# Transposing q and k by 64x64 products in four quarters of the array, and writing the tail of an expert's result row by one-column operations

## The chip, the cores and the metric

One core of one Trainium2 chip runs the kernel. The metric is the time on the device in microseconds (us) for one execution of the whole program: chunked attention, a layer of eight experts of which each token takes one, and a two-layer perceptron.

## The reference, cut to what matters

```python
# q, k, v: (8, 8, 576, 64) f32, standard normal * 0.1; chunks of 64 positions
scores = 64**-0.5 * (q_chunk @ k_chunk.T)          # 64x64 for each batch, head and chunk
attn = exp(scores - rowmax) / (rowsum + 1e-9)
x = (attn @ v_chunk) -> (4608 tokens, 512)         # heads side by side

expert = argmax(norm(x) @ norm(emb).T / tau)       # 8 experts
g = softmax(...)[expert]
x = g * (relu(x @ w1[expert]) @ w2[expert])        # 512 -> 1024 -> 512

h = x @ w_in                                       # 512 -> 2048
out = (h * sigmoid(1.702 * h)) @ w_out             # 2048 -> 512
```

## The kernel before, in words

The program runs through three stages on one core, which overlap a little at their borders.

**Attention (from the start to about 200 us).** The 4608 tokens are 36 tiles of 128; two tiles make a unit of 256 tokens. q and k arrive by unit (`load_qk`), with two neighbouring tokens on one partition, so a partition of a unit's tile holds, for each of 8 heads, 2 tokens of 64 numbers. `emit_T` turns a unit of k (on even steps) or of q (on odd steps) round: 8 f32 transposes of 128x128 on TensorE (L344) fill two PSUM tiles `tp` of tag A, which has two buffers, and four ScalarE copies (L349) of 64 partitions by 512 bring them to `kuT` or `quT`, two copies for each PSUM tile. A loop over steps n then issues, in an order written out by hand, work on several tiles at once. On TensorE a step holds the transposes of the next unit, the gate's products of an earlier tile (L491), the transposes of the attention result (L468), the scores (L371, 16 f32 products of 64x64, in four quarters of the array), the transposes of the probabilities (L394), and the product with v (L416). On ScalarE: the first two copies of L349, a square with row sum (L436), the other two copies, on every second step a copy of 128x1024 (L474), the copy of the transposed probabilities (L401), the exponential (L388). On VectorE: row maximum, subtraction, the division by the row sum (L424 to L428), the scale of the row and its f16 part (L442, L447, L452), the 128x1024 copy on the other steps (L476), and, dripped in between, the gate's small operations. GpSimd forms the rest of the f16 pair (L454, L455). SyncE's queue takes, in order, the loads of q and k, seven steps ahead, those of v, three batches ahead, and the store of the f16 pair (L461, from one of three buffers `xr`).

After the last tiles of a batch group the gate sorts tokens by expert. `find_scales` (L541 to L550) builds for the sorted rows an index `id_i` and a scale `sc_i`, once for the first 3 row tiles (128x3) and once for all (128x40).

**Experts (to about 672 us).** 39 row tiles of 128 sorted tokens are gathered and multiplied with the expert's two matrices, held as f16 pairs. `mm2_evac` (L1069) takes the result `py` out of PSUM: ScalarE sums its squares, VectorE makes a power-of-two scale of the row (L1077 to L1086), ScalarE writes the scaled f16 part (L1089), VectorE the rest (L1090), and beside the row goes a tail of four int32 numbers, which hold the token's index twice (L1078) and the row's scale as an f32 twice (L1093). The tail is written by two operations over 128x2 with a stride of two. The row of 2064 bytes goes to the array `ys` in memory.

**Perceptron (to the end).** The rows of `ys` are multiplied with `w_in` and `w_out` by a scheme of seven block products in place of eight; TensorE runs nearly without a pause.

Of the kernel before, what the change touches and what calls it, by code (L numbers as in the profile page):

```python
# [9 lines left out]
F32 = mybir.dt.float32  # L10
F16 = mybir.dt.float16
BF16 = mybir.dt.bfloat16
I32 = mybir.dt.int32
U32 = mybir.dt.uint32
AF = mybir.ActivationFunctionType
ALU = mybir.AluOpType
# [8 lines left out]
BIAS = 127  # L25
# [3 lines left out]
EXP_BITS = 0x7F800000  # L29
MAN_BITS = 0x007FFFFF  # L30
# [4 lines left out]
def kernel(  # L35
# [13 lines left out]
    nc = tc.nc  # L49
    B, H, S, D = q.shape  # L50
    NT, DM = out.shape
# [4 lines left out]
    HP = H // 2  # L56
# [5 lines left out]
    MAXT = NTILE + NE - 1  # L62
# [7 lines left out]
    const = ctx.enter_context(tc.tile_pool(name="const", bufs=1))  # L70
# [14 lines left out]
    YP = 2 * DM + 8  # L85
# [15 lines left out]
    QR = QU // 128  # L101
# [105 lines left out]
    )  # L207
    id_i = const.tile([128, MAXT], I32, name="id_i")
    sc_i = const.tile([128, MAXT], I32, name="sc_i")

    tau_sb = const.tile([128, 1], F32, name="tau_sb")
    nc.scalar.dma_start(out=tau_sb, in_=tau.partition_broadcast(128))
# [121 lines left out]
    qkT = {}  # L334

    def emit_T(u, nm):

        src = raw.pop((u, nm))
        qkT[u, nm] = att.tile([128, HP, QU], F32, tag=nm + "T", name=nm + "T", bufs=2)
        evacs = []  # L340
        for h2 in range(2):
            p = ps.tile([128, HP, 128], F32, tag="A", name="tp", bufs=2)
            for hp in range(HP):
                nc.tensor.transpose(  # L344
                    p[:, hp, :], src[:, 2 * hp + h2].rearrange("p r d -> p (r d)"), identF
                )
            dst = qkT[u, nm][h2 * 64:(h2 + 1) * 64].rearrange("p hp (c r) -> p hp r c", r=QR)
            evacs.append([
                lambda r=r, p=p, dst=dst: nc.scalar.activation(  # L349
                    out=dst[:, :, r], in_=p[r * 64:(r + 1) * 64], func=AF.Copy  # L350
                )
                for r in range(2)
            ])
        return evacs

# [189 lines left out]
    def scale_of(cols, got, parts_i):  # L545
        nc.vector.tensor_copy(parts_i[:, 0], got[:, 0])
        nc.vector.scalar_tensor_tensor(
            out=parts_i[:, 1], in0=got[:, 1], scalar=1024.0, in1=got[:, 2], op0=ALU.mult, op1=ALU.add
        )
        nc.vector.scalar_tensor_tensor(  # L550
            out=sc_i[:, cols], in0=parts_i[:, 0], scalar=21, in1=parts_i[:, 1],
            op0=ALU.logical_shift_left, op1=ALU.bitwise_or
        )

    def gate(bi):
# [510 lines left out]
    def mm2_evac(i):  # L1066
# [3 lines left out]
        ysq = mo.tile([128, DM], F16, tag="ysq", name="ysq", bufs=1)  # L1070
        s = mo.tile([128, 4], F32, tag="ys", name="ysc", bufs=2)
        si = s.bitcast(I32)
        c_i = sc_i[:, i:i + 1]
        tail = y[:, 2 * DM:YP].bitcast(I32).rearrange("p (a two) -> p a two", two=2)
        n = (YP - 2 * DM) // 4
        nc.scalar.activation(out=ysq, in_=p, func=AF.Square, scale=2.0 ** -20, accum_out=s[:, 0:1])
        nc.vector.tensor_scalar(si[:, 3:4], c_i, EXP_BITS, None, op0=ALU.bitwise_and)  # L1077
        nc.vector.tensor_copy(tail[:, :, 0], id_i[:, i:i + 1].to_broadcast([128, n]))  # L1078
        nc.vector.tensor_scalar(s[:, 0:1], s[:, 0:1], Y_MIN * 2.0 ** -40, None, op0=ALU.max)
        nc.vector.tensor_scalar(  # L1080
            si[:, 1:2], si[:, 0:1], 24, 23, op0=ALU.logical_shift_right, op1=ALU.logical_shift_left
# [1 line left out]
        nc.vector.tensor_scalar(  # L1083
            si[:, 1:2], si[:, 1:2], -1.0, float((BIAS + Y_TOP - 20) << 23), op0=ALU.mult, op1=ALU.add
        )
        nc.vector.scalar_tensor_tensor(  # L1086
            out=si[:, 2:3], in0=c_i, scalar=MAN_BITS, in1=si[:, 1:2], op0=ALU.bitwise_and, op1=ALU.bitwise_or
        )
        nc.scalar.activation(out=y[:, 0:DM], in_=p, func=AF.Copy, scale=s[:, 2:3])  # L1089
        nc.vector.scalar_tensor_tensor(  # L1090
            out=y[:, DM:2 * DM], in0=p, scalar=s[:, 2:3], in1=y[:, 0:DM], op0=ALU.mult, op1=ALU.subtract
        )
        nc.vector.scalar_tensor_tensor(  # L1093
            out=tail[:, :, 1], in0=si[:, 3:4].to_broadcast([128, n]), scalar=float(BIAS << 23),
            in1=si[:, 1:2].to_broadcast([128, n]), op0=ALU.add, op1=ALU.subtract,
        )
        if i < NSURE:
            nc.sync.dma_start(out=ys[i * 128:(i + 1) * 128, :], in_=y)
        elif i < SURE:
# [741 lines left out]
```

## Time and profile before

| | us |
|---|---|
| time, median of 3 runs | 1353.53 (1352.38 to 1356.58) |
| the profiled execution's own time | 1351.38 |
| its span, first to last instruction | 1349.4 |
| busy in the span: TensorE | 1246.7 (92%) |
| VectorE | 1048.0 (78%) |
| ScalarE | 732.8 (54%) |
| GpSimd | 718.4 (53%) |
| mean granted TensorE clock | 0.976 |

The shares are means over stages that differ much: ScalarE is busy for 54% of the whole span, but the slices of the first 150 us show it at eight or nine tenths, and TensorE, at nine tenths from 200 us on, is at seven there. So each part of the change is read in the stage in which its lines run. In the trace a product of two f32 operands stands as two rows on TensorE, a transpose of f32 as one.

### The profile page before, as it was taken

Reading aid. Unit: us, or ns where it says so; the run is one execution under the profiler, and the core shown is the slowest. Engines: PE = TensorE matmul, PEld = TensorE weight load, DVE = VectorE, ACT = ScalarE, POOL = GpSimd, SP = SyncE. Lnnn points to the kernel's source line nnn. Section 1 sums busy time; section 2 is a strip of 40 time slices with the busy share of each in tenths; the row PEclk is TensorE's granted clock in tenths of the full one; section 3 lists DMA queues with packets and bytes.
Section 4 is the critical chain, followed back from the end, with each engine's and each line's share of the span. In section 5 each row is a group of like instructions: output and inputs, shape, how many; then the busy total and the mean of one; then the engine's idle time right before and its main releaser. Section 6 shows DMA issues by size and latency. Waiting matters only on the chain. (4 is left out here: it accounts for less than half of the span.)

```text
span 1349.4 us, 35343 instructions
## 1 busy us (share of the span) xinstructions
PE 1246.7 (92%) x14192; PEld 1027.2 (76%) x14192; DVE 1048.0 (78%) x1872; ACT 732.8 (54%) x1301; POOL 718.4 (53%) x652
## 2 busy tenths in 40 slices
PE   6777767899999999999899999999999999999997
PEld 4666656677676666667588888888888888888886
DVE  4688888878988778886678696968687896968681
ACT  7899855235544545554463645545454645455452
POOL 1455543142444254543167575757667675757664
PEclk9999877999999999999999999999999999999999
DMA  9999635668665759885507162544526062534413
GB/s 197 233 242 230 160 129 131 181 181 229 191 182 174 212 161 274 266 253 133 151 15 212 58 183 99 129 154 94 188 39 226 19 205 77 157 125 125 157 42 116
DMA packets 218454, 213.62 MB, mean 158 GB/s; under 512 B 127320, under 2 KB 171352, under 8 KB 218272
## 3 DMA queue, kind: packets, MB, share of 16 engines
q1 hardware_dynamic: 204880, 184.17, 51.0%
q0 software_dynamic: 6000, 19.67, 4.3%
q10 hardware_dynamic: 7392, 7.36, 1.6%
q8 instruction: 114, 1.87, 0.6%
q14 instruction: 68, 0.56, 0.2%
HBM read 154.98 MB, written 36.52 MB: 142 GB/s over the span
## 5 line engine op out<-in xcount | busy, mean ns | idle before, releaser
L1536 PEld LDWEIGHTS <-wS 128*128 128x128 f16 x3024 | 296.2, 98 | 48.9 <-issue 9.7
L1029 PEld LDWEIGHTS <-w1HL 128*128 128x128 f16 x3744 | 216.9, 99 | 24.1 <-DVEq L962 6.7
L1029 PE MATMUL ph<-xTm,w1HL 128*128 128x128 f16 x3744 | 223.0, 222 | 12.2 <-DVEq L962 5.5
L1064 PE MATMUL py<-w2HL,hT 128*128 128x512 f16 x912 | 203.9, 379 | 6.0 <-DVEq L962 3.4
L1064 PEld LDWEIGHTS <-hT 128*128 128x128 f16 x936 | 89.9, 98 | 109.1 <-issue 8.0
L1089 ACT ACTIVATE y<-py,ysc 128x512 f16<-128x512 f32 x38 | 26.1, 687 | 142.8 <-DVE ysc L1086 142.8
L1004 POOL DMA_INDIRECT xg<-xs,id_i x39 | 44.3, 1135 | 107.6 <-DMA xTm<-xg 70.0
L1536 PEld LDWEIGHTS <-w2HL 128*128 128x128 f16 x864 | 84.6, 98 | 10.6
L1536 PEld LDWEIGHTS <-w1HL 128*128 128x128 f16 x864 | 84.5, 98 | 9.8
L454 POOL TENSOR_TENSOR x<-x,sx_all 128x512 f32<-128x512 f32 x33 | 34.3, 1039 | 107.3 <-DVE rd L424 41.9
L1256 POOL TENSOR_TENSOR wS<-d_f,wS 128x512 f16<-128x512 f32 x28 | 37.0, 1339 | 73.4 <-ACT wS L1255 44.5
L1562 ACT ACTIVATE zA<-zA 128x512 f32<-128x512 f32 x72 | 45.3, 628 | 53.2 <-DVE zA L1559 26.9
L1403 POOL TENSOR_TENSOR w1HL<-zA,w1HL 128x512 f16<-128x512 f32 x36 | 48.5, 1346 | 43.6 <-ACT w1HL L1399 39.7
L1396 DVE TENSOR_TENSOR zA<-zA 128x512 f32<-128x512 f32 x72 | 65.6, 910 | 1.2
L1037 DVE SCALAR_TENSOR_TENSOR hT<-ph,hT 128x512 f16<-128x512 f32 x78 | 51.4, 684 | 14.8 <-ACT hT L1036 14.7
L1036 ACT ACTIVATE hT<-ph 128x512 f16<-128x512 f32 x78 | 44.2, 594 | 30.0 <-PE ph L1029 30.0
L1536 PE MATMUL pd<-stg,wS 128*128 128x256 f16 x456 | 54.5, 272 | 2.2 <-ACT stgB L1399 2.2
L1697 POOL DMA_INDIRECT out_dram<-hT,idc x36 | 35.4, 983 | 35.7 <-ACT hT L1692 32.6
L1536 PE MATMUL pa<-stg,wS 128*128 128x256 f16 x432 | 51.7, 273 | 1.5 <-ACT stgB L1399 1.5
L1090 DVE SCALAR_TENSOR_TENSOR y<-py,ysc,y 128x512 f16<-128x512 f32 x38 | 28.5, 751 | 28.8 <-ACT y L1089 28.8
L1536 PE MATMUL pb<-stg,wS 128*128 128x256 f16 x408 | 48.9, 272 | 1.5 <-ACT stgB L1399 1.5
L349 ACT ACTIVATE kuT<-tp 64x512 f32<-64x512 f32 x72 | 45.2, 628 | 8.8 <-PE tp L344 7.9
(408 smaller groups left out, 3134.4 us busy)
## 6 DMA issues: line engine op xcount, KB each, us to landing
ring<-wod SPq DMA_DIRECT2D x63, 1024.0 KB, 5.1
stg<-in_moe_w_dram SPq DMA_DIRECT2D x14, 1024.0 KB, 6.9
stgB<-in_moe_w_dram SPq DMA_DIRECT2D x14, 1024.0 KB, 6.8
ys<-y SPq DMA_DIRECT2D x39, 258.0 KB, 3.2
vt<-in_v_dram SPq DMA_DIRECT2D x64, 144.0 KB, 5.7
xs<-xr SPq DMA_DIRECT2D x36, 256.0 KB, 5.6
raw_o<-in_moe_w_in_dram SPq DMA_DIRECT2D x16, 512.0 KB, 4.3
raw_o<-in_moe_w_out_dram SPq DMA_DIRECT2D x16, 512.0 KB, 3.8
```

Source lines behind the costliest of these rows:

```text
L349: lambda r=r, p=p, dst=dst: nc.scalar.activation(out=dst[:, :, r], in_=p[r * 64:(r + 1) * 64], func=AF.Copy)
L1004: nc.gpsimd.indirect_dma_start(out=xg[:, :], out_offset=None, in_=src, in_offset=bass.IndirectOffsetOnAxis(ap=id_i[:, i:i + 1], axis=0),)
L1029: nc.tensor.matmul(p[:, f % 4], wt[:, c, fs], xT[:, a, :], start=(c == 0 and a == 0 and wt is w1H), stop=(c == KD - 1 and wt is w1L),)
L1036: nc.scalar.activation(out=hi, in_=p, func=AF.Relu)
L1037: nc.vector.scalar_tensor_tensor(out=lo, in0=p, scalar=0.0, in1=hi, op0=ALU.max, op1=ALU.subtract)
L1064: nc.tensor.matmul(p, hT[:, a, :], wt[:, c, :], start=st, stop=sp)
L1256: nc.gpsimd.tensor_tensor(out=L_, in0=f, in1=H_, op=ALU.subtract)
L1396: nc.vector.tensor_tensor(out=o, in0=x, in1=p, op=op)
L1403: eng.tensor_tensor(out=lo, in0=x, in1=hi, op=ALU.subtract)
L1536: nc.tensor.matmul(dst, lhs(a, k, ab), rhs(b, k), start=first and ab == abs_[0] and k == 0 and m == 0, stop=(k == n - 1 and m == 2), skip_ ...
L1562: nc.scalar.activation(out=z, in_=z, func=AF.Sigmoid, scale=1.702 * 2.0 ** -G_EXP)
L1697: disjoint("out", nc.gpsimd.indirect_dma_start(out=out[:, :], out_offset=bass.IndirectOffsetOnAxis(ap=id_t[j][0][:, 2 * h + t, 0:1], axis= ...
```

## The change

`emit_T` no longer uses transposes. It issues 32 f32 products of 64x64 a unit, each with 64 rows of the source as the operand that is multiplied from the left, transposed, and a 64x64 block of the identity on the right. The source's row half `a` picks the upper or lower half of the array's rows and the PSUM tile; the head's parity `h2` picks the half of its columns and so the half of the PSUM partitions. Both PSUM tiles are requested at the start. Two ScalarE copies of 128 partitions (L356) take the place of the four of 64; they read PSUM with a stride in the innermost dimension and write contiguously, where the old ones read contiguously and wrote with a stride of two. `find_scales` gets three more VectorE operations, which split the scale `sc_i` once for all rows into mantissa (`sc_m`) and exponent (`sc_e`). In `mm2_evac` these columns serve as operands of one-column operations: L1077 goes, L1086 becomes a product by the column `sc_m`, and the tail's two strided operations of two columns become twice two of one column.

```diff
--- before.py
+++ after.py
@@ -207,6 +207,8 @@
     )
     id_i = const.tile([128, MAXT], I32, name="id_i")
     sc_i = const.tile([128, MAXT], I32, name="sc_i")
+    sc_m = const.tile([128, MAXT], I32, name="sc_m")
+    sc_e = const.tile([128, MAXT], F32, name="sc_e")
 
     tau_sb = const.tile([128, 1], F32, name="tau_sb")
     nc.scalar.dma_start(out=tau_sb, in_=tau.partition_broadcast(128))
@@ -338,18 +340,22 @@
         src = raw.pop((u, nm))
         qkT[u, nm] = att.tile([128, HP, QU], F32, tag=nm + "T", name=nm + "T", bufs=2)
         evacs = []
-        for h2 in range(2):
-            p = ps.tile([128, HP, 128], F32, tag="A", name="tp", bufs=2)
-            for hp in range(HP):
-                nc.tensor.transpose(
-                    p[:, hp, :], src[:, 2 * hp + h2].rearrange("p r d -> p (r d)"), identF
+        p = [ps.tile([128, QR, HP, 64], F32, tag="A", name="tp", bufs=2) for _ in range(2)]
+        for hp in range(HP):
+            for r in range(QR):
+                for a in range(2):
+                    rows = slice(a * 64, (a + 1) * 64)
+                    for h2 in range(2):
+                        nc.tensor.matmul(
+                            p[a][h2 * 64:(h2 + 1) * 64, r, hp, :], src[rows, 2 * hp + h2, r, :],
+                            identF[rows, rows], start=True, stop=True,
+                        )
+        for a in range(2):
+            dst = qkT[u, nm][:, :, a * 128:(a + 1) * 128].rearrange("p hp (i r) -> p hp i r", r=QR)
+            evacs.append([
+                lambda a=a, dst=dst: nc.scalar.activation(
+                    out=dst, in_=p[a].rearrange("p r hp i -> p hp i r"), func=AF.Copy
                 )
-            dst = qkT[u, nm][h2 * 64:(h2 + 1) * 64].rearrange("p hp (c r) -> p hp r c", r=QR)
-            evacs.append([
-                lambda r=r, p=p, dst=dst: nc.scalar.activation(
-                    out=dst[:, :, r], in_=p[r * 64:(r + 1) * 64], func=AF.Copy
-                )
-                for r in range(2)
             ])
         return evacs
 
@@ -550,6 +556,13 @@
         nc.vector.scalar_tensor_tensor(
             out=sc_i[:, cols], in0=parts_i[:, 0], scalar=21, in1=parts_i[:, 1],
             op0=ALU.logical_shift_left, op1=ALU.bitwise_or
+        )
+        nc.vector.tensor_scalar(
+            sc_m[:, cols], sc_i[:, cols], MAN_BITS, BIAS << 23, op0=ALU.bitwise_and, op1=ALU.bitwise_or
+        )
+        nc.vector.tensor_scalar(sc_e[:, cols].bitcast(I32), sc_i[:, cols], EXP_BITS, None, op0=ALU.bitwise_and)
+        nc.vector.tensor_scalar(
+            sc_e[:, cols], sc_e[:, cols].bitcast(I32), float(BIAS << 23), None, op0=ALU.add
         )
 
     def gate(bi):
@@ -1070,12 +1083,10 @@
         ysq = mo.tile([128, DM], F16, tag="ysq", name="ysq", bufs=1)
         s = mo.tile([128, 4], F32, tag="ys", name="ysc", bufs=2)
         si = s.bitcast(I32)
-        c_i = sc_i[:, i:i + 1]
-        tail = y[:, 2 * DM:YP].bitcast(I32).rearrange("p (a two) -> p a two", two=2)
-        n = (YP - 2 * DM) // 4
+        tail = y[:, 2 * DM:YP].bitcast(I32)
         nc.scalar.activation(out=ysq, in_=p, func=AF.Square, scale=2.0 ** -20, accum_out=s[:, 0:1])
-        nc.vector.tensor_scalar(si[:, 3:4], c_i, EXP_BITS, None, op0=ALU.bitwise_and)
-        nc.vector.tensor_copy(tail[:, :, 0], id_i[:, i:i + 1].to_broadcast([128, n]))
+        for a in range(0, tail.shape[1], 2):
+            nc.vector.tensor_scalar(tail[:, a:a + 1], id_i[:, i:i + 1], 0, None, op0=ALU.bitwise_or)
         nc.vector.tensor_scalar(s[:, 0:1], s[:, 0:1], Y_MIN * 2.0 ** -40, None, op0=ALU.max)
         nc.vector.tensor_scalar(
             si[:, 1:2], si[:, 0:1], 24, 23, op0=ALU.logical_shift_right, op1=ALU.logical_shift_left
@@ -1083,17 +1094,15 @@
         nc.vector.tensor_scalar(
             si[:, 1:2], si[:, 1:2], -1.0, float((BIAS + Y_TOP - 20) << 23), op0=ALU.mult, op1=ALU.add
         )
-        nc.vector.scalar_tensor_tensor(
-            out=si[:, 2:3], in0=c_i, scalar=MAN_BITS, in1=si[:, 1:2], op0=ALU.bitwise_and, op1=ALU.bitwise_or
-        )
+        nc.vector.tensor_scalar(s[:, 2:3], s[:, 1:2], sc_m[:, i:i + 1].bitcast(F32), None, op0=ALU.mult)
         nc.scalar.activation(out=y[:, 0:DM], in_=p, func=AF.Copy, scale=s[:, 2:3])
         nc.vector.scalar_tensor_tensor(
             out=y[:, DM:2 * DM], in0=p, scalar=s[:, 2:3], in1=y[:, 0:DM], op0=ALU.mult, op1=ALU.subtract
         )
-        nc.vector.scalar_tensor_tensor(
-            out=tail[:, :, 1], in0=si[:, 3:4].to_broadcast([128, n]), scalar=float(BIAS << 23),
-            in1=si[:, 1:2].to_broadcast([128, n]), op0=ALU.add, op1=ALU.subtract,
-        )
+        for a in range(1, tail.shape[1], 2):
+            nc.vector.tensor_scalar(
+                tail[:, a:a + 1], si[:, 1:2], -1.0, sc_e[:, i:i + 1], op0=ALU.mult, op1=ALU.add
+            )
         if i < NSURE:
             nc.sync.dma_start(out=ys[i * 128:(i + 1) * 128, :], in_=y)
         elif i < SURE:
```

On ScalarE's queue, in one step of the attention loop (a step for q, then one for k with its 128x1024 copy), before:

```order
L349 ACTIVATE quT<-tp 64x512 x2
L436 ACTIVATE sq,ss_all<-x 128x512
L349 ACTIVATE quT<-tp 64x512 x2
L401 ACTIVATE PT<-ptp 128x512
L388 ACTIVATE P<-P 128x512
L349 ACTIVATE kuT<-tp 64x512 x2
L436 ACTIVATE sq,ss_all<-x 128x512
L349 ACTIVATE kuT<-tp 64x512 x2
L474 ACTIVATE xTa<-sp_178 128x1024
```

and now:

```order
L356 ACTIVATE quT<-tp 128x4x128
L442 ACTIVATE sq,ss_all<-x 128x512
L356 ACTIVATE quT<-tp 128x4x128
L407 ACTIVATE PT<-ptp 128x512
L394 ACTIVATE P<-P 128x512
L356 ACTIVATE kuT<-tp 128x4x128
L442 ACTIVATE sq,ss_all<-x 128x512
L356 ACTIVATE kuT<-tp 128x4x128
L480 ACTIVATE xTa<-sp_180 128x1024
```

Every pair of copies has become one copy at the same place of the queue; nothing else has moved.

On TensorE's queue, around one unit's turning (the numbers tell apart the buffers), before:

```order
L371 MATMUL sp2_178<-kuT_500,quT_577 64x64 x16
L394 MATMUL ptp_829<-identF_85,P_722 128x128 x4
L416 MATMUL db_179<-vt1_92,PT_738 64x65 x16
L344 MATMUL tp_862<-identF_85,ku_511 128x128 x4
L344 MATMUL tp_867<-identF_85,ku_511 128x128 x4
```

and now:

```order
L377 MATMUL sp2_180<-kuT_430,quT_528 64x64 x16
L400 MATMUL ptp_702<-identF_85,P_593 128x128 x4
L422 MATMUL db_181<-vt0_91,PT_608 64x65 x16
L349 MATMUL tp_734<-identF_85,qu_390 64x64 x2
L349 MATMUL tp_735<-identF_85,qu_390 64x64 x2
L349 MATMUL tp_734<-identF_85,qu_390 64x64 x2
L349 MATMUL tp_735<-identF_85,qu_390 64x64 x2
```

(the last pair of rows stands eight times for a unit). Where one PSUM tile was filled and then the other, the two are now filled in turn, two products at a time, so the first products need both tiles free.

On VectorE's queue, one expert row tile's way out of PSUM, before:

```order
L1077 TENSOR_SCALAR ysc<-sc_i 128x1
L1078 COPY y<-id_i 128x2
L1079 TENSOR_SCALAR ysc<-ysc 128x1
L1080 TENSOR_SCALAR ysc<-ysc 128x1
L1083 TENSOR_SCALAR ysc<-ysc 128x1
L1086 SCALAR_TENSOR_TENSOR ysc<-sc_i,ysc 128x1
L1090 SCALAR_TENSOR_TENSOR y<-py_8698,ysc,y 128x512
L1093 SCALAR_TENSOR_TENSOR y<-ysc 128x2
```

and now:

```order
L1089 TENSOR_SCALAR y<-id_i 128x1 x2
L1090 TENSOR_SCALAR ysc<-ysc 128x1
L1091 TENSOR_SCALAR ysc<-ysc 128x1
L1094 TENSOR_SCALAR ysc<-ysc 128x1
L1097 TENSOR_SCALAR ysc<-ysc,sc_m 128x1
L1099 SCALAR_TENSOR_TENSOR y<-py_8622,ysc,y 128x512
L1103 TENSOR_SCALAR y<-ysc,sc_e 128x1 x2
```

One operation goes ahead of the scale, the two that wrote 128x2 are four of one column, and there are nine operations in place of eight. At the second `find_scales`, once in the program, three operations over 128x40 come in ahead of the evacuation of `hT`, now:

```order
L556 SCALAR_TENSOR_TENSOR sc_i<-got2i 128x40
L560 TENSOR_SCALAR sc_m<-sc_i 128x40
L563 TENSOR_SCALAR sc_e<-sc_i 128x40
L564 TENSOR_SCALAR sc_e<-sc_e 128x40
L1050 SCALAR_TENSOR_TENSOR hT<-ph,hT 128x512 x2
```

## Rows read from the trace of the kernel before

**Rows 1.** The span cut by stage: us, busy of each engine, clock, DMA share, GB/s

```profile
49.00:156.00 107.00, 84.67 (x2058) 67.75 (x2050) 92.08 (x285) 100.10 (x185) 57.59 (x60) 1.00 1.09 235
156.00:206.00 50.00, 31.05 (x643) 26.28 (x634) 41.08 (x131) 31.88 (x61) 23.85 (x25) 0.69 0.35 118
280.00:672.00 392.00, 376.76 (x4169) 272.59 (x4166) 320.79 (x548) 192.44 (x330) 160.72 (x134) 1.00 0.69 200
```

**Rows 2.** DMA of 49 to 156 us, then of 156 to 206: queue, and one issue's landing

```profile
DMA packets 54988, 25.12 MB, mean 235 GB/s; under 512 B 28522, under 2 KB 52120, under 8 KB 54966
...
xs<-xr SPq DMA_DIRECT2D x22, 256.0 KB, 6.4
...
xs<-xr SPq DMA_DIRECT2D x8, 256.0 KB, 2.0
```

**Rows 3.** Waits of 49 to 156 us: total us, times, longest

```profile
PE tp L344 <- ACT quT L349: 8.0, 10, 0.8
...
PE tp L344 <- ACT kuT L349: 6.2, 9, 0.8
DVE xr L452 <- DMA xs<-xr: 5.4, 4, 3.0
```

**Rows 4.** Groups by line, 49 to 156 us: busy us, mean ns | idle before, releaser

```profile
L349 ACT ACTIVATE kuT<-tp 64x512 f32<-64x512 f32 x44 | 27.7, 629 | 0.5
L349 ACT ACTIVATE quT<-tp 64x512 f32<-64x512 f32 x42 | 26.4, 628 | 0.5
...
L401 ACT ACTIVATE PT<-ptp 128x512 f32<-128x512 f32 x22 | 13.1, 595 | 0.6 <-PE ptp L394 0.4
```

**Rows 5.** Line L1261, a ScalarE reader with stride two: ns, minimum, median, maximum

```profile
L1261 ACT ACTIVATE d_t<-raw_o x32: 656/672/689, 265.4 to 599.7; 128x512 f32<-128x512 f32 x32
```

**Rows 6.** The span cut into 20 us (columns as in Rows 1)

```profile
80.00:100.00 20.00, 15.22 (x376) 12.17 (x374) 15.89 (x51) 17.87 (x35) 13.71 (x16) 1.00 1.12 245
100.00:120.00 20.00, 15.58 (x370) 12.45 (x371) 17.84 (x58) 19.31 (x36) 8.81 (x8) 1.00 1.15 252
```

**Rows 7.** Timeline, 155 to 192 us: start, us, instruction [idle before]

```profile
159.55 0.21 PE L596 MATMUL gb<-g_oh,tri 128*128 128x64 f16 x1 [3.37 <-DVE g_oh L586]
...
162.01 1.95 PE L344 MATMUL tp<-identF,ku 128*128 128x128 f32 x8
...
166.85 1.09 PE L344 MATMUL tp<-identF,qu 128*128 128x128 f32 x8
...
169.12 0.69 PE L371 MATMUL sp<-kuT,quT 64*64 64x64 f32 x32
```

**Rows 8.** Timeline, second scales: start, us, instruction [idle before]

```profile
265.08 0.26 DVE L550 SCALAR_TENSOR_TENSOR sc_i<-got2i 128x40 int32<-128x40 int32 x1
...
266.65 1.66 PE L1029 MATMUL ph<-xTm,w1HL 128*128 128x128 f16 x21 [1.65 <-DVEq L962]
```

**Rows 9.** Tile ysc, one-column operation: ns, minimum, median, maximum

```profile
L1079 DVE TENSOR_SCALAR ysc<-ysc x39: 139/146/155, 242.0 to 665.1; 128x1 f32<-128x1 f32 x39
```

**Rows 10.** Line L1078 (columns as in Rows 9)

```profile
L1078 DVE COPY y<-id_i x39: 153/159/4056, 242.0 to 661.6; 128x2 int32<-128x2 int32 x39
```

**Rows 11.** Groups by line, 280 to 672 us (columns as in Rows 4)

```profile
L1078 DVE COPY y<-id_i 128x2 int32<-128x2 int32 x35 | 24.0, 687 | 0.0
```

**Rows 12.** Timeline, evacuation after a change of weights: start, us, instruction [idle before]

```profile
552.03 0.62 DVE L1078 COPY y<-id_i 128x2 int32<-128x2 int32 x1
...
553.12 0.32 DVE L1086 SCALAR_TENSOR_TENSOR ysc<-sc_i,ysc 128x1 int32<-128x1 int32 x1
...
555.24 0.29 PE L1029 MATMUL ph<-xTm,w1HL 128*128 128x128 f16 x2 [1.91 <-ACTq L962]
```

**Rows 13.** Waits of 280 to 672 us: total us, times, longest

```profile
PE ph L1029 <- DVEq L962: 3.9, 6, 0.8
PE ph L1029 <- ACTq L962: 3.4, 3, 1.9
...
PE py L1064 <- DVEq L962: 3.4, 4, 1.1
```

## The prediction, made before the changed kernel ran

> **What bounds the kernel now.** I read the table of stages first, then for the stages touched the groups by line, the transfers and the waits. From 49 to 156 us ScalarE is busy for 100.10 of 107 us, VectorE for 92.08, TensorE for 84.67, at a granted clock of 1.00 [rows 1]: the reader is to see that ScalarE sets the pace there, and that two others stand close behind it. Behind these stands a third limit. In the same 107 us the queues move 25.12 MB at 235 GB/s, and a store of 256 KB lands after 6.4 us, where in the next stage it takes 2.0 [rows 2]: the transfers are queued up, and VectorE waits four times, once for 3.0 us, until an earlier store has freed the buffer that it writes [rows 3]. From 280 to 672 us TensorE is busy for 376.76 of 392 us [rows 1], and only what ends its waits is worth time. What moves less than 0.3%, some 4.06 us, can't be told from no change; so 1349.47 and 1357.59 are the borders of "same".
>
> **The copies.** Removed in 49 to 156 us: 44 and 42 copies at 629 and 628 ns, 54.1 us of ScalarE, or 1.257 us a pair [rows 4]. Added: 43 copies of 128 partitions over the same 512 columns. No row shows one with their stride. Below, a copy of PSUM of the same size without stride takes 595 ns [rows 4]; above, a ScalarE read with a stride of two takes 672 [rows 5]. That the old ones, with a strided write and half the partitions, took 629 tells that partitions are free and strides cheap. I take 610, nearest to the row that has the same source and size: 43 x 0.610 = 26.2 us, so ScalarE is relieved of 27.9 us (25.2 to 28.5). Its 100.10 falls to 72, and it is no longer the bound.
>
> What is late next decides the gain. VectorE keeps its 92.08 us, so not more than 14.9 us can go. The transfers keep their 25.12 MB: at the 245 GB/s of the 20 us from 80 to 100 us they take 102.5 us, at the 252 of the next 20, 99.7 [rows 6], against 107 now. Loads are issued seven steps ahead and stand behind stores and v in SyncE's queue, so a faster step asks earlier for the same bytes, and only the empty places between them can be filled. The stage's gain thus lies between 0 (235 GB/s is all that this mix of small pieces gives) and 7.3 us (252 throughout). I take 245, the stretch in which ScalarE was busy least, 17.87 of 20 us: 25.12 / 0.245 = 102.5, a gain of 4.4 us. The buffers of the stores let the computation end somewhat closer to the last load; I take 1.0 us, between 0 and the longest wait of 3.0.
>
> **The products on TensorE.** A unit's eight transposes took 1.09 us; 32 rows of 64x64 products, the same quarters in turn, took 0.69 [rows 7]. A product f32 is two rows, so the 32 new ones are 64 rows. Twice 0.69 is the upper bound, 1.38 us. The lower: one product alone lasts 0.21 [rows 7], the other 0.48 are eight groups of four rows at 0.06; 0.21 + 16 x 0.06 = 1.17. I take 1.17: 0.08 more a unit, with some 22 units 1.8 us (to 6.4) on an engine that idles for 22.3 of 107 us. Of that idle time 8.0 and 6.2 us ended with a copy of L349 [rows 3], which now ends earlier; the first products of a unit do need both PSUM tiles, but the second tile's copy is over 0.65 us sooner, more than the half turn of 0.55 that now starts behind it. Cost nothing while VectorE or the queue paces; 1.8 to 6.4 us if TensorE did.
>
> **156 to 206 us.** Here the clock is 0.69 and VectorE busy 41.08 of 50 us, ScalarE 31.88 [rows 1]: the copies are off the path. A unit's turn at the low clock takes 1.95 us [rows 7]; by 1.17/1.09 it grows by 0.14, twice: +0.3. The three scale operations over 128x3, 0.15 each, fall into VectorE's 8.9 idle us.
>
> **find_scales over 128x40.** Three operations beside L550's 0.26 us stand ahead of the L1037 for which TensorE then waits 1.65 us [rows 8]. A wait of that kind is lengthened by all of them: 3 x 0.18 = +0.5 us (0.45 to 0.8; 0 if another releases it).
>
> **The evacuation.** L1078 has a median of 159 ns and a maximum of 4056, in 280 to 672 us a mean of 687: 24.0 - 35 x 0.159 = 18.4 us of VectorE in stretched copies; the one-column L1079 never took over 155 in 39 [rows 9, 10, 11]. The new tail has the one-column form, so the stretches go and three small ones are added after the row. That is worth TensorE's time only where it waits for VectorE. After a change of weights it does: the copy took 0.62 and L1086 0.32 ahead of the scaled row, and the next product came 1.91 us late [rows 12]. There 0.46 + 0.16 us go; I count that place and one like it without L1086's part, 0.46: -1.1. Against it: ahead of the scale two operations stand where two stood, behind the row two for one, 0.15 us more; at seven changes of expert that is 1.0, of which I take half, since not each waits: +0.5. Net -0.6. The upper bound of a gain is all that TensorE waits there for these queues, 3.9 + 3.4 + 3.4 = 10.7 us [rows 13]; the bound of a loss 1.0.
>
> The Trainium skill, "SBUF — State Buffer", section Who interferes with whom, speaks against this part: it lists the tensor_scalar among the operations that can take the pair of ports shared with GpSimd and be blocked for a whole instruction. By that rule the new operations would be stretched like the copy and the -1.1 would be lost; the 39 rows of L1079 with a maximum of 155 ns do not bear it out for one column.
>
> **Sum.** -4.4 - 1.0 + 0.3 + 0.5 - 0.6 = -5.2 us, and nothing in the last stage, whose code is the same. The profiled execution of 1351.38 would become 1346.2; the median of the runs is 2.15 above the profiled time, so the forecast is 1348.3 us.
>
> **Rivals.**
> 1. *The queue takes it all.* 235 GB/s is what the queue gives with 28522 of 54988 packets under 512 bytes [rows 2]; ScalarE then simply waits for VectorE, and VectorE for the stores. For it: the landing of 6.4 us. Against: 245 and 252 in slices with the same work. Only +0.3 + 0.5 - 0.6 and up to 1 us are left: about 1352.7. Chance 0.25.
> 2. *VectorE sets the pace and the queue yields.* The step shortens until VectorE, 92.08 us, fills the stage but for some 5 us, as ScalarE now but for 6.9: 107 - 97 = 10 us, with the small terms 1343.5. For it: the queue may be full only because loads are asked for seven steps ahead. Against: the wait for stores. Chance 0.17.
> 3. *The clock of 156 to 206 us rises.* Its fall follows pauses of TensorE, as the 3.37 us at 159.55 [rows 7]. If products in the place of transposes kept it up, 0.62 of the stretch, the share that a mean of 0.69 between levels of 1 and 0.5 gives, would go at the upper level: 0.62 x 31.05 = 19.3 us busy become 10.8 by 1.95/1.09. Half of the 8.5 lies on the path: -4.2, so 1344.1. Against: the pauses that end with VectorE stay. Chance 0.05. The Trainium skill, "TensorE: Matmul & The Clock Gate", Part 4: PE-mode transpose, says that transposes do not count as busy for the clock, which would make this so; the trace's clock of 1.00 from 49 to 156 us, with eight transposes and more a step, lies against its strength.
> 4. *Slower: the clock of 49 to 156 us falls.* With ScalarE out of the way TensorE's short waits may run together into longer ones, for VectorE or a late load, as those before 159.55. At the low level its rows last 1.79 times as long (1.95 for 1.09). Its 22.3 idle us are used up once a third of the stage is at that level (84.67 x 0.79 x 0.33 = 22); from there each further tenth costs 6.7 us. At half the stage: 33.4 - 22.3 = +11, 1364. For it: the next stage does just this. Against: 1.00 now, and a shorter step gives denser work. Chance 0.08.
> 5. *The change does not do what it says.* If PSUM read with a stride in the innermost place made a copy cost 1.04 us or more, ScalarE would win under 10 us and the queue's gain shrink to about nothing: 1353. Against: 672 ns for the other stride. Chance 0.05.
>
> **How the numbers follow.** The forecast has 0.40, with a range of its own of 1345 to 1351.5 (the term of the queue between -7 and -1.5). Faster than 1349.47: 0.7 of its 0.40, rivals 2 and 3, 0.22, together 0.50. Same: 0.3 of 0.40, nearly all of rivals 1 and 5, 0.26: 0.38. Slower: rival 4 with tails of 1 and 5, 0.12. The range of 8 in 10: 1341.5 below, where half of rival 2 is left out, to 1355.5 above, where rival 4 and some of 1 are.
>
> **What would show it.** In the profile after: one copy a PSUM tile of 595 to 672 ns, 43 in the stage; ScalarE busy under 80 us in 49 to 156 and waiting for VectorE or TensorE; the end of the stage 4 to 6 us earlier with 240 to 250 GB/s; the turn of a unit at 1.17 to 1.38 us; more waits of VectorE for stores than 5.4 us; one-column tails that never exceed 160 ns; VectorE's busy time in the expert stage some 25 us lower with TensorE's waits nearly as before. The forecast is wrong if GB/s stay at 235 (rival 1), if the stage shortens by 8 us or more (rival 2), or if the clock of either stage differs by over 0.05 (rivals 3 and 4).

## The result, and the profile after

The changed kernel took 1365.67 us (median of four runs, 1360.17 to 1368.15) against 1355.05 before (1352.38 to 1357.32): a ratio of 1.0073 with a 95% interval of 1.0047 to 1.0099, so some 10 us slower. The forecast was 1348.3, between 1341.5 and 1355.5, faster at 0.50. It was wrong in sign. The profile shown below is of the fastest of the four runs (1360.17 us), 5.5 us under their median, so it shows rather less of the loss than a middle run would.

The table of stages of the changed kernel, whose columns are those of [rows 1], for the main part of the attention, for its end and for the expert stage:

```profile
49.00:156.00 107.00, 81.08 (x2832) 69.50 (x2831) 79.30 (x243) 64.14 (x129) 51.85 (x56) 0.90 0.92 212
156.00:206.00 50.00, 34.12 (x1165) 29.59 (x1165) 42.08 (x144) 25.89 (x52) 21.20 (x23) 0.86 0.31 91
...
280.00:672.00 392.00, 376.34 (x4220) 271.34 (x4221) 299.79 (x592) 192.04 (x327) 160.66 (x135) 1.00 0.73 209
```

ScalarE fell from 100.10 to 64.14 us of 107 [rows 1]. But VectorE fell too, from 92.08 to 79.30, the transfers from 235 to 212 GB/s: in the same 107 us the kernel did less of its work, and no engine is near its limit. 39 of the new copies stand in these 107 us where 43 pairs of the old ones stood; for the work of 43 ScalarE would take some 71 us, an estimate from these two numbers. The groups by line of this stage (busy us, mean ns | idle before, releaser) show the copies and what TensorE did:

```profile
L422 PE MATMUL db<-vt,PT 64*64 64x65 f32 x608 | 16.1, 245 | 5.4 <-issue 4.7 <-DVE x L434 0.7
L377 PE MATMUL sp<-kuT,quT 64*64 64x64 f32 x608 | 15.3, 238 | 6.4 <-issue 6.4
L349 PE MATMUL tp<-identF,ku 64*64 64x64 f32 x640 | 14.3, 239 | 2.2 <-issue 2.2
...
L349 PE MATMUL tp<-identF,qu 64*64 64x64 f32 x576 | 12.4, 230 | 3.9 <-issue 3.2 <-ACT kuT L356 0.7
...
L356 ACT ACTIVATE quT<-tp 128x512 f32<-128x512 f32 x20 | 11.9, 594 | 2.7 <-PE tp L349 2.6
L356 ACT ACTIVATE kuT<-tp 128x512 f32<-128x512 f32 x19 | 11.2, 587 | 5.8 <-PE tp L349 5.7
```

A copy of 128 partitions takes 587 and 594 ns, two of the old ones took 1257 [rows 4]. Where TensorE waited for these copies before, 8.0 and 6.2 us [rows 3], it now waits for "issue": for nothing that the profile shows. The waits of TensorE from 0 to 215 us (total us, times, longest):

```profile
PE tp L349 <- issue: 9.5, 9, 1.9
PE db L422 <- issue: 7.2, 6, 2.1
PE sp L377 <- issue: 6.4, 3, 2.6
PE ptp L400 <- issue: 3.1, 1, 3.1
PE gb L497 <- issue: 1.7, 1, 1.7
```

27.9 us in all. They fall on five different lines, the new products and old ones alike, and in the middle of a line's products. This is one of them in the timeline (start, us, instruction): a step's 32 score rows, which run for 0.69 us in one piece in [rows 7], stop after 19 of them for 2.61 us.

```profile
82.16 0.56 PE L377 MATMUL sp<-kuT,quT 64*64 64x64 f32 x19
85.32 0.45 PE L377 MATMUL sp<-kuT,quT 64*64 64x64 f32 x13 [2.61 <-issue]
85.33 0.31 PEld L377 LDWEIGHTS sp<-kuT,quT 64*64 64x64 f32 x12 [2.74 <-issue]
```

What ends them shows when all of TensorE's rows of the trace (products, weight loads and the rows of its sequencer) are counted from the start of the program. Each of the 15 pauses over 0.8 us in which it waited for issue comes at the same remainder of that count to 256, give or take one row. Nine of them:

```
goes on at us   pause us   rows since the last one listed
        36.6      1.9
        42.1      2.1        256
        52.6      2.4        512
        74.5      1.7       1280
        79.9      1.8        256
        85.3      2.6        256
        95.4      1.7        512
       114.7      3.1       1024
       124.8      1.7        512
```

From 30 to 215 us there are 21 pauses over 0.8 us in all, and these 15 stand at that remainder; before there are 22, and no remainder has more than two. The page of the profile lists a queue for instructions. Its row in the changed kernel (packets, MB, share):

```profile
q8 instruction: 129, 2.11, 0.7%
```

and in the kernel before:

```profile
q8 instruction: 114, 1.87, 0.6%
```

Each packet has 16384 bytes, 64 for each of 256 instructions. One of them starts at 82.5 us and lands at 83.7; TensorE goes on at 85.3. So it is in all 15 pauses: TensorE goes on 1.3 to 1.8 us after such a packet has landed. TensorE's program comes in pages of 256 instructions, it had used up one before the next was there, and waited. Between 30 and 150 us a page was fetched every 4.78 us in the mean (single ones 3.5 us apart), before every 6.89. In this stretch TensorE crosses into a new page 25 times, and each time exactly one page has been fetched since the crossing before: no more than one is held ahead. The trace also shows where the 4.78 us go. By the medians a fetch starts 2.0 us after a crossing, its packet takes 1.3 us, and a TensorE that stands waiting goes on 1.5 us after the landing. The Trainium skill, "Runtime: NRT & Kernel Launch", section Instruction fetch mechanics, gives the same page of 16 KiB or 256 instructions, and holds that fetching is mostly hidden; the first agrees with this trace, the second does not here.

Why more instructions: the whole page counts 16208 products of TensorE where 14192 were, 2016 more, each with its weight load: 4032 instructions over 36 units, 112 a unit. The last score product starts at 214.3 us (199.6 before), the first expert row is scaled 14.8 us later, the last expert row 10.6 later, the program ends 9.0 later in the profiled executions: 15 us lost in the attention, and in these two profiles some 4 won back in the experts.

In the expert rows the new operations never meet a stretch (tile ysc, then L1089: ns, minimum, median, maximum):

```profile
L1103 DVE TENSOR_SCALAR y<-ysc,sc_e x78: 202/205/207, 258.9 to 677.9; 128x1 int32<-128x1 int32 x78
...
L1097 DVE TENSOR_SCALAR ysc<-ysc,sc_m x39: 213/214/215, 257.3 to 676.2; 128x1 f32<-128x1 f32 x39
```

```profile
L1089 DVE TENSOR_SCALAR y<-id_i x78: 136/146/157, 256.6 to 672.1; 128x1 int32<-128x1 int32 x78
```

VectorE has 21 us less to do from 280 to 672 us, 299.79 for 320.79 [rows 1]. Those that take a column as their second operand last 205 and 214 ns, not 150.

### The profile page after: what moved, and what is told of

The parts are those of the page before. It is cut to its first block, busy times and chain, and to the rows that moved or that the text cites. A ratio compares the mean times of both kernels' runs of the same rounds, so it can differ in the third digit from the quotient of the medians.

```text
span 1358.4 us, 39310 instructions
## 1 busy us (share of the span) xinstructions
PE 1250.9 (92%) x16208; PEld 1038.9 (76%) x16208; DVE 1025.6 (76%) x1917; ACT 685.6 (50%) x1229; POOL 718.1 (53%) x652
## 5 line engine op out<-in xcount | busy, mean ns | idle before, releaser
L1042 PEld LDWEIGHTS <-w1HL 128*128 128x128 f16 x3744 | 213.2, 98 | 22.7 <-DVEq L975 8.4
L1042 PE MATMUL ph<-xTm,w1HL 128*128 128x128 f16 x3744 | 218.9, 220 | 11.5 <-DVEq L975 7.4
L1077 PE MATMUL py<-w2HL,hT 128*128 128x512 f16 x912 | 204.3, 379 | 5.9 <-DVEq L975 2.3
L1077 PEld LDWEIGHTS <-hT 128*128 128x128 f16 x936 | 89.9, 98 | 109.2 <-issue 8.5
L1545 PEld LDWEIGHTS <-w1HL 128*128 128x128 f16 x864 | 84.6, 98 | 9.8
L1050 DVE SCALAR_TENSOR_TENSOR hT<-ph,hT 128x512 f16<-128x512 f32 x78 | 51.6, 686 | 26.7 <-ACT hT L1049 26.6
L1412 POOL TENSOR_TENSOR w1HL<-zA,w1HL 128x512 f16<-128x512 f32 x36 | 48.5, 1348 | 41.7 <-ACT w1HL L1408 41.7
L384 DVE TENSOR_REDUCE mx<-sp 128x8 f32<-128x512 f32 x36 | 24.8, 688 | 47.0 <-PE sp L377 47.0
```

Of the source, the lines that this page charges most:

```text
L1042: nc.tensor.matmul(p[:, f % 4], wt[:, c, fs], xT[:, a, :], start=(c == 0 and a == 0 and wt is w1H), stop=(c == KD - 1 and wt is w1L),)
L1050: nc.vector.scalar_tensor_tensor(out=lo, in0=p, scalar=0.0, in1=hi, op0=ALU.max, op1=ALU.subtract)
L1077: nc.tensor.matmul(p, hT[:, a, :], wt[:, c, :], start=st, stop=sp)
L1412: eng.tensor_tensor(out=lo, in0=x, in1=hi, op=ALU.subtract)
L1545: nc.tensor.matmul(dst, lhs(a, k, ab), rhs(b, k), start=first and ab == abs_[0] and k == 0 and m == 0, stop=(k == n - 1 and m == 2), skip_ ...
```

## The experiments

Theory I: instruction pages; the new turn has too many instructions for their supply. Theory P: the products themselves, by their quarters, by the two PSUM tiles that they hold at once, or by the clock. Theory E: the new expert rows are at fault. Theory Q is the forecast's own third limit, the data queue. Experiments that were timed together share the runs of the kernel before; a gain or loss in us is the ratio's distance from one, times their median. "Last scores" is the start of the last score product in the profiled execution (199.6 us before).

**1. The attention's part alone.** Against the changed kernel:

```diff
-    sc_m, sc_e and their three operations in find_scales; one-column tail in mm2_evac
+    find_scales and mm2_evac as before
```

> The products and the 128-partition copies alone, the expert rows as before. Theory I (instruction pages): TensorE now gets 128 instructions a unit for the turn where it got 16, and its stream comes in pages of 256 instructions that arrive more slowly than it uses them; its pauses put down to 'issue' stand at whole multiples of 256 instructions after one another. The last scores end about 15 us later than before (199.9), the whole time is 13 to 16 us over before. Theory E (expert rows): if the new tail and scales were at fault, this kernel would be 4 to 8 us faster than before, as forecast.

1371.62 us, ratio 1.0141 (1.0117 to 1.0164): 19 us slower, last scores at 218.9. TensorE's waits from 0 to 215 us:

```profile
PE tp L347 <- issue: 13.9, 12, 2.5
PE sp L375 <- issue: 9.8, 4, 4.5
PE db L420 <- issue: 7.5, 7, 1.8
```

15 of its 20 pauses over 0.8 us stand at one remainder to 256, the same as in the changed kernel. The loss lies here. It is larger than theory I had said, and in the profile 4 us more than the changed kernel's, whose attention has the same code; one pause of 4.5 us is the plainest difference. Which run was profiled explains much of these 4 us (this one lies 1.7 us under its median, the changed kernel's 5.5), but not why the medians differ; that was not found.

**2. The rows' part alone.** Against the changed kernel:

```diff
-    emit_T: 32 products of 64x64, two copies of 128 partitions
+    emit_T: 8 transposes of 128x128, four copies of 64 partitions
```

> The expert rows and scale columns alone, the turn by transposes as before. Theory I: nothing of the loss is here; the stretched copies go, 4 to 5 us are gained between the first and the last row tile, 1349 to 1351. Theory E: 8 to 12 us slower than before. The forecast's own term: 0.1 us faster.

1350.92 us, ratio 0.9984 (0.9972 to 0.9996): 2.2 us faster, by the interval 0.5 to 3.8. From the scaling of the first expert row to that of the last it took 420.6 us, before 423.0: a gain in the place where theory I had it, but half of the 4 to 5 us expected. Theory E falls.

**3 and 4. The products for k alone, for q alone.**

```diff
-        (the products)
+        if nm == "ku":          # experiment 4: "qu"
+            (the products, two copies)
+        else:
+            (the transposes, four copies)
```

> The changed kernel, with the products for k alone; q by transposes and four copies as before. A pair of steps has then 144 instructions for turning in place of 32 (before) or 256 (changed). Theory I: about 240 instructions a step against 300, at some 50 a us 4.8 us a step: the pages keep up, ScalarE is relieved by half, and attention ends at or ahead of before: last scores at 195 to 201 us, time 1341 to 1350. Theory P (the products themselves cost the time, by the quarters, the two tiles held at once or the clock): half of the loss stays, last scores at about 207 us, time about 1357.

> The same with the products for q alone, k by transposes. Steps that turn k carry the 128x1024 copy on ScalarE, steps that turn q do not, so the relief falls on the lighter step. Theory I: pages keep up as in the half for k, but the gain is smaller, last scores at 197 to 202 us, time 1344 to 1351. Theory P: last scores at about 207 us, time about 1357.

For k: 1353.09 us, ratio 0.9999 (0.9980 to 1.0018), last scores at 201.9. For q: 1357.08, ratio 1.0026 (1.0014 to 1.0037), last scores at 210.3. Both missed: theory I had both gain, theory P had both at about 207. The waits of the kernel with q alone:

```profile
PE db L437 <- issue: 7.4, 5, 2.5
PE sp L392 <- issue: 5.7, 3, 2.4
PE tp L350 <- issue: 1.9, 3, 1.1
```

With one smaller wait that is 15.6 us; with k alone it is 8.5. The mean over two steps, by which I had reckoned, is not what counts when no more than one page is held ahead: a step of some 300 instructions is held up, and one of 184 beside it can't lend it time. With k alone the heavy stream falls on the step that ScalarE's 128x1024 copy makes long anyway; with q alone it falls on the short one. That reading fits both and was not tested apart.

**5 and 6. The same TensorE time, many instructions or few.** Both are edits of the kernel before.

```diff
 # experiment 5, emit_S
-        for hp in range(HP):
+        for hp in [i for _ in range(3) for i in range(HP)]:
 # experiment 6, emit_T and emit_PT
-            for hp in range(HP):
+            for hp in [i for _ in range(2) for i in range(HP)]:
-        for hp in range(HP):
+        for hp in [0, 1, 0, 1, 2, 3]:
```

> The kernel before, with the 16 score products of each step issued three times over into the same place: 128 instructions more a step for TensorE and about 1.4 us (two times 0.69), nothing else. Theory I (instruction pages): over 300 instructions a step, at the changed kernel's 5.0 to 5.8 us for them; pauses put down to issue at multiples of 256; last scores at 214 to 230 us as in the changed kernel or later, time 1367 to 1385. A theory by TensorE's time alone: 5.2 us a step where 5.0 were, last scores at 203 to 210, time about 1360, and no pauses of issue.

> The kernel before, with ten more 128x128 transposes a step (each unit turned twice over, two of the four transposes of the probabilities repeated): the same 1.4 us of TensorE as the score products issued thrice, but 20 instructions where these are 128. Theory I: no pauses of issue, last scores at 203 to 212 us, at least 8 us ahead of the kernel with the scores issued thrice. TensorE's time alone: the same as that kernel within 3 us.

Experiment 5: 1385.81 us, ratio 1.0241 (1.0224 to 1.0258), 33 us slower, last scores at 234.8, just over the far end of what theory I had said. Its waits:

```profile
PE sp L371 <- issue: 12.3, 11, 2.5
PE db L416 <- issue: 8.2, 6, 2.3
```

11 of its 14 pauses over 0.8 us stand at one remainder to 256, give or take two rows. Its stage:

```profile
49.00:156.00 107.00, 86.53 (x2733) 74.49 (x2723) 72.58 (x218) 82.57 (x151) 45.00 (x46) 0.97 0.90 207
```

Experiment 6: 1352.83, ratio 0.9997 (0.9981 to 1.0014), last scores at 202.0, no wait for issue. Its stage:

```profile
49.00:156.00 107.00, 103.91 (x2238) 91.56 (x2229) 92.17 (x284) 100.49 (x185) 56.81 (x59) 1.00 1.10 236
```

TensorE is at 103.91 of 107 us, 19.2 more than before [rows 1], and nothing is lost; with the instructions it is 33 us. In these two kernels `emit_T`'s copies, the tiles and the ScalarE load are those of before. This decides for the number of instructions, and against TensorE's time. It doesn't clear the form of the product, since experiment 5 adds quartered ones. What clears it is the count: the pauses come at the same remainder to 256 whether the next row is a quartered product (L371, L416), a 128x128 transpose (one of L344 here, one of L400 in the changed kernel) or a product of the gate (L497 there).

**7. The turn kept, other instructions taken away.** An edit of the changed kernel.

```diff
 def emit_S(t):
     u, tt = divmod(t, QR)
+    if t >= 2:
+        return
```

> The changed kernel, with the scores computed for the first two tiles alone; later tiles use those, so the attention is left out in part, and tokens go to other experts: only the attention stage is compared, by the last product with v. TensorE gets 64 instructions and 0.69 us a step less; the turning products and their copies stay. Theory I: 235 instructions a step, 4.6 to 4.8 us, the pauses of issue fall from about 28 us to under 8, and the last product with v ends at 200 to 212 us (before 214, changed 228). Theory P (the turning products themselves): pauses stay, the last product with v ends after 222.

1353.09 us, a time that can't be compared, as tokens go to other experts. The last product with v starts at 210.7 us, where it was 214.0 before and 228.1 in the changed kernel:

```profile
L424 PE MATMUL db<-vt,PT x1152: 217/218/367, 25.0 to 210.7; 64*64 64x65 f32 x192
```

All the loss of the attention is gone with 64 instructions a step less, with all the quartered turning products and both tiles in place. The scores' time on TensorE and the waits for them went too; experiment 6 speaks against the first, the second was not tested apart. Of waits for issue 15.7 us are left, twice what I had said, 13.3 of them before turning products; the five over 0.8 us stand at the same remainder to 256.

**8. Less data beside the pages.** An edit of the changed kernel, in `issue_v`.

```diff
-            nc.sync.dma_start(out=dst, in_=src)
+            if v_n[0] < H * NV:
+                nc.sync.dma_start(out=dst, in_=src)
```

> The changed kernel, with v loaded for the first three of eight batches alone (the others use these): 40 loads of 144 KB of 256-byte pieces are left out, about a quarter of the bytes and half the packets of the attention stage. Theory I with pages that stand behind data: a page comes sooner, the stage from 49 us on loses 5 to 12 of its 15 us. Theory I with a fixed time for a page: last scores within 3 us of the changed kernel's 214.7. Theory Q (the data queue is the bound, in both kernels): the stage ends 15 us earlier or more, ahead of the kernel before.

1360.73 us, ratio 1.0051 (1.0034 to 1.0068), last scores at 215.3. The stage:

```profile
49.00:156.00 107.00, 83.62 (x2906) 71.92 (x2908) 78.18 (x239) 63.42 (x127) 51.02 (x54) 0.89 0.63 168
```

The share of the DMA engines fell from 0.92 to 0.63, and a page still came every 4.79 us (4.78). The pages are not slow because data stand in front of them, and the queue does not pace the changed kernel.

**9 and 10. Half the instructions, more TensorE time.** For k alone, or for k and q:

```diff
-  nc.tensor.matmul(p[a][h2 * 64:(h2 + 1) * 64, r, hp, :], src[rows, 2 * hp + h2, r, :], identF[rows, rows], ...)
+  nc.tensor.matmul(p[h2 * 64:(h2 + 1) * 64, hp, :], src[:, 2 * hp + h2, c, :], identF, ...)
```

> The changed kernel, with k turned by 16 products of all 128 rows, 64 columns wide, against the 128x128 identity: the same two copies of 128 partitions, but 64 instructions a unit in place of 128; q by transposes and four copies as before. TensorE works about 1.9 us on such a unit in place of 1.17. Theory I: a page of 256 instructions takes some 4.8 us whatever the data load, so a step of 235 instructions needs 4.4 to 4.6 us and is no longer held up: few pauses of issue (under 4 us), last scores at 193 to 198 us (before 199.9, rows alone 196.7), time 1344 to 1350. Theory P: as the half for k with 64x64 products, last scores 202 or later, time 1353 or more.

> The same for k and for q: every step has about 235 instructions for TensorE, against 300 in the changed kernel, and its ScalarE is relieved as fully as in the changed kernel. Theory I: 4.6 to 4.9 us a step, by the pages and by TensorE's own 4.7; pauses of issue under 10 us; last scores at 190 to 200 us, time 1340 to 1352. Theory P: the loss stays, last scores after 208.

Experiment 9: 1350.71 us, ratio 0.9973 (0.9961 to 0.9986), last scores at 201.0, waits for issue 1.0 us. Experiment 10: 1350.91, ratio 0.9973 (0.9962 to 0.9984), last scores at 202.8. The stage of experiment 10:

```profile
49.00:156.00 107.00, 102.30 (x2578) 88.21 (x2576) 91.10 (x281) 72.05 (x142) 56.28 (x58) 0.99 1.08 238
```

The waits for issue are down to 1.9 us, as theory I had it, and the loss is gone. But the attention ends no earlier than before, and later than theory I had said for either (193 to 198 and 190 to 200): in experiment 10 TensorE is now busy for 102.30 of 107 us. Both are as fast as the rows alone within their intervals and beat the kernel before and the changed one; no more than the gain of the rows is seen.

**11. The queue in the kernel before.** The same edit of `issue_v` as in experiment 8, in the kernel before.

> The kernel before, with v loaded for the first three batches alone (the output differs from there on). Theory Q, the forecast's third limit: if the data queue paced the kernel before together with ScalarE, VectorE's waits for the stores go and the last scores end 4 to 10 us earlier. Otherwise, ScalarE alone pacing: 199.9 within 2 us.

1350.26 us, ratio 0.9972 (0.9960 to 0.9985); last scores at 196.8. DMA share 0.68 for 1.09, and 3.8 us gained (2.0 to 5.4). The last scores moved by 2.8 us, which meets neither reading (4 to 10, or within 2); in experiment 2, whose attention is that of before, they start at 196.4, so that much is scatter between runs. The queue has at most a small part in the pace, below what theory Q wanted.

**12. The relief without pages in the way.** An edit of the changed kernel.

```diff
-            for r in range(QR):
+            for r in range(1):
...
-                out=dst, in_=p[a].rearrange("p r hp i -> p hp i r"), func=AF.Copy
+                out=dst, in_=p[a][:, 0].unsqueeze(3).to_broadcast([128, HP, 64, QR]), func=AF.Copy
```

> The changed kernel, with only the first of each two neighbouring tokens of q and k turned; the copies, of the same size, write its column for both (the attention differs from the reference). 16 products and 64 instructions a unit in place of 32 and 128, some 0.7 us of TensorE in place of 1.17, about 235 instructions a step: neither pages nor TensorE are in the way, and ScalarE is relieved in full. The forecast's own term, a gain of 4.4 to 5.4 us in the attention stage once ScalarE no longer paces: last scores at 191 to 196 us, time 1344 to 1348 with the 2 to 3 us of the rows. If VectorE, the gate's steps and the short hand-overs pace as closely as ScalarE: last scores at 196 to 200, time 1349 to 1352, as the rows alone.

1347.40 us (1343.29 to 1351.60), ratio 0.9937 (0.9913 to 0.9961), 8.5 us faster than before and 6.3 beyond the rows alone; by the two intervals, 3.3 and 1.6 us to each side, some 3 to 10. Its stage, then the waits before the turning products, from 0 to 206 us:

```profile
49.00:156.00 107.00, 81.72 (x2480) 67.75 (x2482) 87.98 (x276) 67.63 (x137) 56.27 (x58) 0.88 1.05 231
```

```profile
L349 PE MATMUL tp<-identF,ku 64*64 64x64 f32 x576 | 17.9, 254 | 17.8 <-DMA ku<-in_k_dram 12.6 <-issue 2.8 <-ACT quT L356 2.4
L349 PE MATMUL tp<-identF,qu 64*64 64x64 f32 x576 | 17.7, 249 | 3.9 <-ACT kuT L356 2.7 <-issue 1.1
```

By the times, relieving ScalarE would be worth what the forecast said, if TensorE can be fed. The trace does not show it. The profiled execution is one of the longer ones of its runs (1351.21 us, last scores at 201.1, 12.6 us of waits for the first loads where it was 10.1 before), and between 49 and 156 us its steps, from one step's first score product to the next one's, take 5.0 us in the mean, where the kernel before takes 4.9. As in experiment 7, the attention differs and tokens may go to other experts, so part of the 8.5 us may lie elsewhere.

## Why the prediction was wrong, point by point

- **The copies: right.** 594 and 587 ns, where 610 was taken. ScalarE's 64.14 us are for less work; for the same work some 71 us, where 72 was forecast.
- **The products on TensorE: the step that failed.** The prediction counted them as 64 rows, priced their time as 1.17 us a unit (in 49 to 156 us 19 units took 26.7 us, 1.41 each) and set their cost at "nothing while VectorE or the queue paces". TensorE's time does cost nothing: experiment 6 adds 19.2 us of it to the stage for a ratio of 0.9997. What was not priced is that each row has a weight load and each is an instruction to be fetched, so that the unit brings 128 instructions in place of 16. At a page of 256 every 4.8 us, some 53 a us, a step that had 184 (scores 64, product with v 64, transposes 24, gate 16, turn 16) now has 296, and takes 296 / 53 = 5.6 us in the mean. So it is: between 49 and 156 us the steps of the scores take 5.6 us, where they took 4.9. The row for it was there: the instruction queue of the page and the counts of TensorE's rows.
- **What is late next: not VectorE, not the queue.** Both were named as the limit behind ScalarE; VectorE was at 79.30 of 107 us and the queue slower than before. Neither came into play. Whether the term of -4.4 to -5.4 us was right stays open: the times of experiment 12 agree with it (6.3, some 3 to 10), the trace of that run and experiments 9 and 10 show no shorter attention. The changed kernel could not collect it.
- **The rival on the slower side** took the clock. The clock of 49 to 156 us did fall, from 1.00 to 0.90, and that of 156 to 206 us is 0.86 where it was 0.69. It is not the cause: experiment 5 loses 33 us at 0.97, and experiment 12 gains 8.5 us with 0.88 in its stage. TensorE's pauses come first, and the clock falls with them: in the changed kernel each of the five stretches at the lower level, 1.2 GHz, that begin between 36 and 156 us (41.7, 52.0, 86.1, 96.3 and 113.4 us) begins while TensorE stands waiting for issue or within 1 us after. What the clock adds to the loss was not measured apart. By the prediction's own arithmetic the kernel would have lost nothing at that clock, its idle time taking it up.
- **The evacuation: right in sign, too small in size.** -0.6 was forecast for the rows, with +0.5 for `find_scales`; measured are -2.2 us (-0.5 to -3.8) for both. The stretched copies are gone as said; none of 78 one-column operations of L1089 lasts over 157 ns, as the rows of L1079 had let expect [rows 9]. Those with a column as second operand go over the 160 ns that were named as a limit (L1103 to 207), but they don't stretch. The three operations of `find_scales` cost what was said: the evacuation of `hT` starts 0.64 us after L556, where it was 0.18 after L550 [rows 8], 0.46 us for a forecast of 0.5. The product behind it waits 2.60 us for 1.65; the other 0.5 us lies ahead of the scales and is not explained. The Trainium skill, "SBUF — State Buffer", section Who interferes with whom, counts tensor_scalar among the operations that can contend with GpSimd when their operands meet certain conditions; no run here shows that for one column.

The line of the kernel before that [rows 8] does not show, and those of the changed kernel:

```profile
265.26 1.27 DVE L1037 SCALAR_TENSOR_TENSOR hT<-ph,hT 128x512 f16<-128x512 f32 x2
```

```profile
280.50 0.20 DVE L556 SCALAR_TENSOR_TENSOR sc_i<-got2i 128x40 int32<-128x40 int32 x1
...
281.14 1.28 DVE L1050 SCALAR_TENSOR_TENSOR hT<-ph,hT 128x512 f16<-128x512 f32 x2
...
282.53 1.68 PE L1042 MATMUL ph<-xTm,w1HL 128*128 128x128 f16 x27 [2.60 <-DVEq L975]
```

- **Left open.** The parts measured apart, +19.1 and -2.2 us, don't add up to the whole, +9.9 (6.4 to 13.4). The kernel with the attention's part alone lost 4 us more in the attention than the changed kernel, with the same code there. And the 4.8 us of a page are seen in their parts, but not why a fetch starts some 2 us after the crossing and why TensorE goes on only 1.5 us after the landing; that it is not the load of data is shown. Rival 2's 1343.5 leaves out the small terms that it names (with them 1343.7), which changes nothing.

## What to carry to other kernels

Price a change of TensorE's form by its instructions as well as by its time: products and weight loads in each step, against pages of 256 that here came no faster, in the mean, than one in about 4.8 us. Splitting a product into four quarters, and an f32 product in two rows, multiplies that number. When idle time is put down to "issue", count the rows between the pauses; a constant step of 256 names the cause. And look at the supply step by step: with one page held ahead a light step should not pay for a heavy one, which fits experiments 3 and 4 but was not tested apart.

## What the runs showed of the hardware that was not expected

- Where its work asks for more than some 53 instructions a us in the mean, TensorE stands still for 0.8 to 4.5 us at a page's end: 15 of 21 pauses over 0.8 us at one remainder to 256, and 11 of 14 in experiment 5. One page is fetched for each crossing, after the crossing (median 2.0 us), and a waiting TensorE goes on 1.3 to 1.8 us after it has landed. With 0.63 of the DMA engines busy in place of 0.92 the pages came no faster (4.79 and 4.78 us).
- A one-column VectorE operation with a column of numbers as its second operand lasts 205 to 214 ns in the median, one with constants 144 to 154.
- A ScalarE copy that reads PSUM with a large stride in the innermost place and writes without a gap is no slower than a plain one: 587 to 594 ns for 128x512, against 595 [rows 4]. The other way round, plain reading and strided writing, 632 to 636 ns in experiment 10.
